# Transposes of two batches moved to SyncE's DMA queue, under a new written order

## The chip, the cores and the metric

The kernel runs on one core of one Trainium2 chip. The metric is the device time of one execution in microseconds: 173.79 us before the change (median of 3 runs, 173.76 to 174.22). Engines: PE is TensorE's matmul, PEld its weight load, DVE is VectorE, ACT is ScalarE, POOL is GpSimd, SP is SyncE. SyncE computes nothing here; all loads and stores are issued on its queue (SPq).

## The reference

Four batches, 8 heads, 768 positions, 48 values a head. A gated linear recurrence is followed by a mixer with a low-rank position part and a channel part:

```python
for t in range(S):                                   # per batch and head, state is 48 x 48
    state = alpha[:, :, t, :, None] * state + np.einsum('bhd,bhe->bhde', k[:, :, t], v[:, :, t])
    y[:, :, t] = np.einsum('bhd,bhde->bhe', q[:, :, t], state)
x = y as (4, 768, 384)
h = xt @ U @ V                                       # xt: x transposed, U 768 x 32, V 32 x 768
u = x + h.transpose(0, 2, 1)
out = u + np.maximum(u @ w_ch1, 0.0) @ w_ch2         # w_ch1 384 x 1536, w_ch2 1536 x 384
```

Inputs and output are float32; the kernel multiplies in bfloat16 and sums in float32 in PSUM.

## The kernel before

A batch's 768 positions are cut into six chunks of 128. Batch 0 and the first four chunks of batch 1 go through `stage_pair`, which takes two chunks together by halves of the heads; the last two chunks of batch 1 and all chunks of batches 2 and 3 go through `stage_gla`. One chunk in `stage_gla` runs like this:

- Four loads of 192 KB (alpha, k, q, v) into four of 36 `io` buffers, each load in runs of 192 bytes (L347).
- ScalarE takes the logarithm of alpha (L543). PE forms its cumulative sum over the chunk (L550) and the chunk's total (L552). ScalarE takes exponentials of minus and plus the sum, `ai` and `aa` (L560, L561), and of the total, `tot` (L563).
- GpSimd makes `rk` = k times `ai` and `rq` = q times `aa` (L570), 128 positions by 8 heads by 64 columns in bfloat16 (48 used, the rest zero), and casts v to `rv`.
- PE transposes `rk` and `rq` in four 128 x 128 blocks each (L583) into one PSUM bank each, and ScalarE or VectorE copies the banks to `kt` and `qt` in SBUF (L590).
- PE forms the scores from `kt` and `qt` (L608), VectorE masks them to `pm` (L618). PE forms the chunk's own state (L631), VectorE adds the previous state and VectorE or GpSimd scales the sum by `tot` (L658, L642).
- PE forms the output from `qt` with the previous state and from `pm` with `rv` (L670, L675), and it is copied to `xb`.

After six chunks `stage_mix` makes the low-rank part (L691, L722) and transposes the sum `ub` for the channel part (L732). `mlp1` multiplies by the first weight matrix in 24 groups of three matmuls a batch (L759), each group followed by the maximum with zero on ScalarE or VectorE into `h1t` (L769, L771). `mlp2` multiplies by the second, for each chunk in three groups of four matmuls (L782); then VectorE adds `ub` into one of four `ou` buffers (L789) and SyncE stores it (L790). PE groups of one batch's channel part stand between those of the next batch's recurrence.

The order of all work is written out by hand in `TABLE`: three characters an entry, two for the operation and one for its engine. `Plan.run` walks the table, binds a buffer to each operation that needs one (that which the plan takes to come free first), and issues the operation on the engine named. Each engine runs its own entries strictly in this order, and waits at an entry until its inputs and its buffer are there. The costs in `Plan.add` (`{"SP": 1100.0}`), `LAT` and `lag` serve only to estimate when buffers come free, and to decide how many idle matmuls (L286, `filler`) are put between PE's groups in the first 28 us. They choose buffers and do not delay anything.

`QUEUE_T` is a list of (batch, chunk) whose transposes are done by a transfer instead of PE. It is empty before the change; the code for it issued on ScalarE's queue.

Of the kernel before, what the change touches and what calls it, by code (L numbers as in the profile page):

```python
# [20 lines left out]
BdSAgSBeSBbSAmSA0SAsSGMGANGAJGALGAVGBgSAXGDRDDXDAuSAySCrPAwSD8ADvPBfSAqSBkSA2SCtDCsDDSDD+PEQPDzABlSDwAEIAESAEADD-DEBPEWP
EPPERAECPEXPBhSBmSDYPETPGLADxAEYDEDDGNPEEPDaAGhAG3AEVDEUDEZPEFDDZDGOAEGAEbAEaDG5PEcPEdPBiSEeDEfPEiPGjPBjSEuPElPEvPEjPErP
EmPG7AG6AGPAG8AHOAGQAEwAEsPGSDE3PEoPGUPEgPE4DBnSEpPGWDGRDBsSEkAEtAE7PHQPBoSEqAEnAHTAHRAGkAE8DGlAE1PE5PFpPE6DFqAHSAEhDFnP
GTPFdPFPPFRPFQAFSAGnDFeDFDPGVDEzPFHPGmAFIAGXPGoDFoDGaPE0DGbDGcDFbPFFPGpPGqPGsAGrAFEDFcDE2DAjGG+GGYDG9DGZDFfPFgAFVPFZPFTP
FrPAZGFGAGiAFXPE-PFWAFUDFaAFYDFsDGePGwPGtPE9PGgDFAAE+AG4AGxDGyDGuDFJPFjPHUDFNPHAPFBPGzDHCAGfDGvDAnGFKAFkAFCAHVGFlPAlAHlA
AhGApGG-PFhPHXPHBDG0PHGPAzGAvGFmDA1GArGHZAFOAAtAGdDG1AHHDF3PFLPFMAFiDHIDHJDG2AHWPFyPHYDHaPHDPAxAHnPA3GHPAFzPF4PHrAH7AHoA
HpAH9PH+AIAGHqAHEDHcDHbDHFDF8PH-AHdPHLPF0PF5PHsGIBGHtGHNDHeDHfDF1DHgDF6DHmGHKGHuPICPF9PIDPGBPHhDIEDIFAHwDHMDHvPHiPIGPHxD
HyPGCPHkAH8GHjDKBAJtAH0DHzDH1PH3DH2DH4GGGPGDPH5PF+PKDPIIDIHDIJPGHPJvPIKABpSJxAJzAJwABqSKFAH6DF-DGEDB0SF2SBvSBwSJyABrSF7S
B8SB1SBtSB2SBxSBzSBySILPBuSIMDExPFtPJ0GJ1GEyDITPIVPINPIbPGIPIPPJuGIWDFuPIZPIUDIODIQDIXPIRPIcDIaDISDFvPIdPJ2PIYAIfPIhPIzP
KEAIeAKrAKHAKWAFwDKGAI0AJ4DIgDJHPJ3PKtPJDPJIAI5PJ5DGJDKvALVAJ9PKYPIrPKxAKuAKwAJ+DKCGKIGKzGKXGI3PJ6PI6DJEDIiAKaAKZAI7PJFP  # L30
I-PKcAKbAJ8DI4DJ7DKRPI9PI8DI+AJ-PKdGJNPInPJGDJADKSDJODIsAKKPJLPItPJMAKMAIuDKTDLXPK1PIxPKyGKeGK3DLZAKJGLYAJBPKmPIjPJCAKAA
IpPIkDIoDK0PKfPKgPJjPKLPJkPK2DKhAIyAIqAKiDKnDKNAK4PK5DK6DKjPKOPJoPB3SB4SB9SJJPB+SGKSCASB5SLAAB6SGASJKAKPDKlDKoDKkDLaGKsG
LbGB7SCFSCISB-SCESLCPJpPIlPJlPJqPLGALEALFALDAImDJmDKQDLHGLdPJePLIGLfALcPK7PK+PI1PKUPK8DI2AKVDLJPJfPLKPKpPNHALeAKqALLDK-A
JrDLMDK9GLBGJgPNJPLQPLgPLNPLRDLODLPDLiDJUPIvPJZPJVPLTPLSGLWGLhDLjPNwANbAIwDLUDLkANyPJaPNdPLlPNhANfANLANeANNANKANMANzAJnS
JsSCGSCCSNjGCBSCQSN1ACDSGFSN0AN2ANgALmDCJSJbPJPPJcDJhDLtPCKSCMSCUSCHSNPGNiGCWSCPSCLSCNSNOGNIGN4GN3GNcGJQPLnPOGGLvPJWPLpP
LuDLoDLwDLzPL1PNlPLqDLxPNRPLrPJRPL0DL2DLsANkPL3PNQPLyDNmDMLPL4DNTDNnANSAJSDMNPL5PNXPMPPMVPMODL6DNYDMQAMMAOaAMWAOvACVSCOS
CRSNUPNoPNWDMdPMDPNqDNpDN5PL-PMhPMEDMeAOFAMAAMiDNVDOxPOHPOcPN7AOzAOeAOyAOdAOfAN6PMRPMJPMHPN8DMKAOJAOKANrPMXPOgAOIAMSDMYD
MIDNsDNxGOLAMnPO1GL7PL9PNtDL+AN9PL8AMBPMfPNZPO3PN+DN-DMoAO5DNaDOAPNuPMFPODPMCANvAMgAMGDOBDOCDOEDCSSJiSO0GOMGONGOhGOVPMuP
O2POPPOOPMvPMZPOiGOjPORAO4AOQAMaAOkPOWDJXDMTPOlDOmDO6POSPOnPMUAMwPJTSCTSCXSObGOXDOqPO8DOpDOrDOTDOoDO7DMzPMbPM0PMxDOUDOsG
OwGM4POtPNCPO9POYPO+AMlPMjPOuDOZAMcAO-PMkAMmDM5PPAAMpPPHPPBPPJPPNPMqPM1PPCDPIDPDPPKDPODPPPPEDNDPPLPFxSMySPQDJYSPFPM6PPRP  # L40
# [128 lines left out]
def kernel(  # L169
# [164 lines left out]
    def stage_loads(b):  # L334
        def load(t, src, c, key):
            if paired(b, c):
                hs, sl = slice((c % 2) * HP, (c % 2 + 1) * HP), slice((c // 2) * 2 * C, (c // 2 + 1) * 2 * C)
# [9 lines left out]
            P.add({"SP": 1100.0}, lambda e: nc.sync.dma_start(t(), src[b, :, sl, :].rearrange("h t d -> t h d")), w=[t], prio=key)  # L347
# [427 lines left out]
    def mlp2(b, ub, h1, c):  # L775
# [13 lines left out]
        P.add({"DVE": 468}, lambda e: nc.vector.tensor_tensor(ou(), ub()[:, c, :], hb()[:, 0:DM], op=ALU.add), r=[hb, (ub, c)], w=[ou], prio=-100)  # L789
        P.add({"SP": 550.0}, lambda e: nc.sync.dma_start(out[b, c * C : (c + 1) * C, :], ou()), r=[ou], prio=-1)  # L790
# [53 lines left out]
```

## Time and profile before

| | |
|---|---|
| median of 3 runs | 173.79 us |
| the profiled execution, its own time | 173.62 us |
| its span | 171.8 us |
| PE busy | 156.7 us, 91% of the span |
| DVE, ACT, POOL busy | 117.6, 89.5, 62.4 us |
| DMA queue of the loads and stores | 28.52 MB in 87104 packets, 66.2% of 16 engines |
| last matmul ends | 161.0 us |

The time is about 1.8 us above the span, which runs from the first to the last instruction. "Busy" of PE counts pipelined matmuls with modelled ends. A stage view gives the busy time of each engine between two points of the span; a chain row gives a start, a length and the work that ended the wait before it.

### The profile page before, as it was taken

The numbers are of one execution on the slowest core, as the hardware profiler recorded it, in microseconds if no ns is written. First come the engines' busy times: TensorE is split into PE (matmuls) and PEld (weight loads), VectorE is DVE, ScalarE is ACT, GpSimd is POOL, SyncE is SP. The second block draws the span as 40 slices with busy tenths as digits, with TensorE's granted clock in tenths as the row PEclk, the third lists the DMA queues.
The fourth block names the chain that finished last, engine by engine and source line by source line (L and its number), as shares of the span: only waits on it lengthen the run. The fifth ranks groups of instructions, "written<-read, shape, count | busy, mean of one in ns | idle before, by whom it ended". The sixth has DMA issues, their size and how long they took to land.

```text
span 171.8 us, 4668 instructions
## 1 busy us (share of the span) xinstructions
PE 156.7 (91%) x1814; PEld 102.8 (60%) x1814; DVE 117.6 (68%) x257; ACT 89.5 (52%) x226; POOL 62.4 (36%) x101
## 2 busy tenths in 40 slices
...
GB/s 135 283 303 311 259 287 270 320 349 325 291 179 196 218 236 177 222 255 173 59 50 132 237 164 191 239 191 4 0 92 4 90 1 0 4 137 0 47 92 183
DMA packets 87126, 28.81 MB, mean 168 GB/s; under 512 B 80928, under 2 KB 87072, under 8 KB 87104
## 3 DMA queue, kind: packets, MB, share of 16 engines
q1 hardware_dynamic: 87104, 28.52, 66.2%
...
q14 instruction: 8, 0.07, 0.1%
HBM read 23.79 MB, written 4.72 MB: 166 GB/s over the span
## 4 chain that ended last, share of the span: by engine, by line
PE 79%; DVE 9%; DMA 5%; issue 2%; SPq 1%; ACT 1%; DVEq 0%
PE ps L782 28%; PE ps L759 22%; PE ps L583 4%; PE ps L415 3%; DMA io<-in_alpha_dram 3%; PE ps L722 2%; DMA out_dram<-ou 2%; DVE pm L453 2%; PE ps L608 2%; PE ps L442 2%; DVE h1t L771 2%; PE ps L732 2%; PE ps L675 2%; PE ps L528 1%; PE ps L550 1%
## 5 line engine op out<-in xcount | busy, mean ns | idle before, releaser
L782 PE MATMUL ps<-w_sb,h1t 128*128 128x384 bf16 x288 | 54.2, 326 | 0.0
L759 PE MATMUL ps<-uT,w_sb 128*128 128x384 bf16 x288 | 53.0, 326 | 0.2 <-DVE pm L453 0.2
L759 PEld LDWEIGHTS <-w_sb 128*128 128x128 bf16 x288 | 26.7, 98 | 16.1 <-issue 0.3
L782 PEld LDWEIGHTS <-h1t 128*128 128x128 bf16 x288 | 26.2, 98 | 15.7 <-issue 0.6
L769 ACT ACTIVATE h1t<-ps 128x384 bf16<-128x384 f32 x56 | 25.4, 503 | 19.0 <-PE ps L759 17.0
L771 DVE TENSOR_SCALAR h1t<-ps 128x384 bf16<-128x384 f32 x40 | 20.9, 550 | 12.4 <-PE ps L759 12.2
L789 DVE TENSOR_TENSOR ou<-ub,ps 128x384 f32<-128x384 bf16 x24 | 12.5, 548 | 14.8 <-PE ps L782 11.9
L570 POOL TENSOR_TENSOR rk<-io,ai 128x384 bf16<-128x384 f32 x14 | 13.0, 939 | 16.9 <-ACT ai L560 16.9
L618 DVE TENSOR_TENSOR pm<-ps,maskc 128x512 bf16<-128x512 f32 x28 | 18.0, 683 | 1.5 <-PE ps L608 1.5
L570 POOL TENSOR_TENSOR rq<-io,aa 128x384 bf16<-128x384 f32 x14 | 12.9, 928 | 8.5 <-ACT aa L561 8.5
L297 POOL CAST w_sb<-io 128x384 bf16<-128x384 f32 x21 | 11.9, 591 | 7.7 <-DMA io<-in_moe_w_ch_dram 5.3
L293 ACT CAST xb<-ps 128x192 bf16<-128x192 f32 (+1 forms) x18 | 6.8, 397 | 14.5 <-PE ps L675 13.2
L723 DVE TENSOR_TENSOR ub<-xb,ps 128x384 bf16<-128x384 bf16 x24 | 11.9, 548 | 3.2 <-PE ps L722 3.0
L453 DVE TENSOR_TENSOR pm<-ps,maskp 128x512 bf16<-128x512 f32 x20 | 13.0, 680 | 1.0 <-PE ps L442 1.0
L293 ACT COPY qt<-ps 128x512 bf16<-128x512 bf16 x12 | 8.2, 682 | 9.2 <-PE ps L583 5.9
L297 POOL CAST rv<-io 128x384 bf16<-128x384 f32 x17 | 8.7, 513 | 5.0 <-DMA io<-in_v_dram 5.0
L293 ACT COPY uT<-ps 128x768 bf16<-128x768 bf16 x5 | 4.0, 799 | 9.1 <-PE ps L732 9.0
L293 ACT COPY kt<-ps 128x512 bf16<-128x512 bf16 x13 | 7.5, 588 | 1.2 <-PE ps L583 0.9
L642 POOL TENSOR_TENSOR st<-sm,tot 128x384 bf16<-128x384 f32 x4 | 3.3, 831 | 12.4 <-DVE sm L658 12.4
L295 DVE CAST xb<-ps 128x192 bf16<-128x192 f32 (+1 forms) x16 | 6.6, 423 | 1.6 <-PE ps L528 1.0
L286 PE MATMUL ps<-filler 128*128 128x512 bf16 x20 | 6.5, 461 | 1.2 <-DVE filler L217 1.2
L372 ACT ACTIVATE lt<-io 128x384 bf16<-128x384 f32 x10 | 5.0, 535 | 4.2 <-DMA io<-in_alpha_dram 4.2
(116 smaller groups left out, 252.7 us busy)
## 6 DMA issues: line engine op xcount, KB each, us to landing
io<-in_q_dram SPq DMA_DIRECT2D x24, 192.0 KB, 4.1
io<-in_alpha_dram SPq DMA_DIRECT2D x24, 192.0 KB, 3.9
io<-in_v_dram SPq DMA_DIRECT2D x24, 192.0 KB, 3.7
io<-in_k_dram SPq DMA_DIRECT2D x24, 192.0 KB, 4.1
io<-in_moe_w_ch_dram SPq DMA_DIRECT2D x24, 192.0 KB, 4.1
out_dram<-ou SPq DMA_DIRECT2D x24, 192.0 KB, 2.1
...
```

The lines of the kernel that those rows point to most:

```text
L293: nc.scalar.copy(dst, src)
L297: nc.gpsimd.tensor_copy(dst, src)
L453: nc.vector.tensor_tensor(dst, s2, maskp.to_broadcast([C, 2, 2, C]), op=ALU.mult)
L570: eng.tensor_tensor(dst()[:, :, 0:D], a(), x(), op=ALU.mult)
L583: nc.tensor.matmul(t[:, p, :], lhsT=ring()[:, 2 * p : 2 * p + 2, :].rearrange("t h w -> t (h w)"), rhs=ident, start=True, stop=True, is_tr ...
L618: nc.vector.tensor_tensor(pm()[:, :, par, :], s2, maskc.to_broadcast([C, HP, C]), op=ALU.mult)
L723: P.add({"DVE": 465}, lambda e, c=c, hb=hb: nc.vector.tensor_tensor(ub()[:, c, :], xb()[:, c, :], hb()[:, 0:DM], op=ALU.add), r=[hb] + xk( ...
L759: nc.tensor.matmul(hb()[:, 0:TW], lhsT=w1_sb[:, ct, jt * 128 : (jt + 1) * 128], rhs=uT()[:, ct, tt * TW : (tt + 1) * TW], start=(ct == 0), ...
L769: nc.scalar.activation(dst, hb()[:, 0:TW], AF.Relu)
L771: nc.vector.tensor_scalar_max(dst, hb()[:, 0:TW], 0.0)
L782: nc.tensor.matmul(hb()[:, 0:DM], lhsT=h1()[:, jt, c * C : (c + 1) * C], rhs=w2_sb[:, jt, :], start=(jt == 0), stop=(jt == NJ - 1),)
L789: P.add({"DVE": 468}, lambda e: nc.vector.tensor_tensor(ou(), ub()[:, c, :], hb()[:, 0:DM], op=ALU.add), r=[hb, (ub, c)], w=[ou], prio=-100)
```

## The change

The rows of `TABLE` are all new. `QUEUE_T` names the twelve chunks of batches 2 and 3, and for each of them two transposing transfers (`rk` to `kt`, `rq` to `qt`, each 128 x 512 values) are issued on SyncE's queue, in place of two PE groups of four transposes and two copies out of PSUM. `Op` gets a field `iss`, the queue time that the plan books for an entry on SyncE, and some planning figures of loads and stores differ. The new table has 24 entries more on SyncE and 48 fewer on PE, ScalarE and VectorE together.

```diff
 TABLE = """
-A6SA4SA8SBASBESABSA+SA-SA9SA5SBISBMSBGSA7SBCSBFSBHSBBSBDSBKSBJSCuACYACaPBNSBOSBLSCwPADGDbADEACbACdACyAC1DDGPDdPAEPCxACcA
...
+A4SBASBA6SBBSBYSA7SA5SA8SBCSA9SBESBaSA-SBZSBDSA+SBISABSBGSBMSBFSBHSBNSBOSBJSBKSBLSCYADEADGPCaPBPSDIACZGCcACdAG3ADHACbADJA
...
-    __slots__ = ("engs", "fn", "prio", "deps", "bufs", "n", "users", "est", "i", "mode", "lag")
+    __slots__ = ("engs", "fn", "prio", "deps", "bufs", "n", "users", "est", "i", "mode", "lag", "iss")
...
             if eng == "SP":
-                dma = max(dma, t + 600.0) + cost
-                clock[eng] = max(t + 550.0, dma - 3500.0)
+                dma = max(dma, t + op.iss + 30.0) + cost
+                clock[eng] = max(t + op.iss, dma - 3500.0)
                 end = dma + 2000.0
...
-    QUEUE_T = ()
+    QUEUE_T = tuple((b, c) for b in (2,3) for c in range(6))
...
-                    {"SP": 775.0},
+                    {"SP": 690.0},
...
-            P.add({"SP": 1100.0}, lambda e: nc.sync.dma_start(t(), src[b, :, sl, :].rearrange("h t d -> t h d")), w=[t], prio=key)
+            P.add({"SP": 930.0}, lambda e: nc.sync.dma_start(t(), src[b, :, sl, :].rearrange("h t d -> t h d")), w=[t], prio=key)
...
         if (b, c) in QUEUE_T:
             for dst, src in ((kT, rk), (qT, rq)):
-                P.add({"ACT": 100}, lambda e, dst=dst, src=src: nc.scalar.dma_start_transpose(dst(), src().rearrange("t h w -> t (h w)")), r=[src], w=[dst], prio=pr + 18, lag=2600)
+                P.add({"SP": 450}, lambda e, dst=dst, src=src: nc.sync.dma_start_transpose(dst(), src().rearrange("t h w -> t (h w)")), r=[src], w=[dst], prio=pr + 18, lag=-700.0, iss=1250.0)
...
-        P.add({"SP": 550.0}, lambda e: nc.sync.dma_start(out[b, c * C : (c + 1) * C, :], ou()), r=[ou], prio=-1)
+        P.add({"SP": 550.0}, lambda e: nc.sync.dma_start(out[b, c * C : (c + 1) * C, :], ou()), r=[ou], prio=-1, lag=-1500.0)
```

Where the text speaks of the written order, these parts of the two tables are meant (each entry: batch, chunk; for the matmuls of `mlp2` also the group, 0 to 2; line numbers are those of the kernel before, from L44 on one more than in the changed file):

| | before | after |
|---|---|---|
| PE's last groups of `mlp2` | ... 3,2 g1; 3,5 g1; 3,4 g1; 3,2 g2; 3,0 g1; 3,5 g2; 3,0 g2; 3,4 g2 | ... 3,1 g1; 3,0 g0; 3,4 g2; 3,1 g2; 3,5 g0; 3,0 g1; 3,3 g1; 3,3 g2; 3,0 g2; 3,5 g1; 3,5 g2; 3,2 g1; 3,2 g2 |
| VectorE's last additions L789 | 3,4; 2,4; 3,1; 3,3; 3,0; 3,2; 3,5 | 3,4; 3,1; 3,0; 3,5; 3,3; 3,2 |
| SyncE's last stores | 3,4; 3,0; 3,1; 3,5; 2,4; 3,2; 3,3 | 2,4; 3,1; 3,4; 2,0; 3,0; 3,5; 3,3; 3,2 |
| SyncE's entries from the third load of batch 2 on | 46 loads, 9 stores up to the last load | 45 loads, 8 stores, 24 transfers up to the last transfer |
| PE groups between the cumulative sum and the scores of 3,4 | 12 of L759, 2 of L782, 16 of the recurrence | 3 of L759, 7 of L782, 7 of the recurrence |

More of the change, by code (lines that the diff above doesn't have):

```diff
@@ L16 @@
 TABLE = """
-A6SA4SA8SBASBESABSA+SA-SA9SA5SBISBMSBGSA7SBCSBFSBHSBBSBDSBKSBJSCuACYACaPBNSBOSBLSCwPADGDbADEACbACdACyAC1DDGPDdPAEPCxACcA
-C3PBPSC5DCfDC0GCeGCzACvABQSBYSBUSAaSChPAGPC2PDIADeADJAAFADHADyADgADfACgPAHDC9PD0PCjDC+DCiDC4AEHADiGCZGC6PAcSAASBSSASSBcS
-AQSAeSCnPDkPC-PDhGAOSBRSC7DCoDDADC8DDKGDFGD1AD2ADmADcAD3ACkPCpPDjPDqPEJPDlADrPDLDClDCqDDsDCmDD5DDBPELAEKADCAEMADMPDtPDNP
-DnPD4GDTPEOGENGDDADuDDpDDUPD7PDVDDoDDOADPAD9ADQPDWPD6PACGAISBWSAbGBVSBTSAMSAYSAKSAfGAdGAkSAWSBXSBZSATGARGAPGAUSBaSAiSAoS
@@ L21 @@
[L21 to L40, printed above, removed]
@@ L41 @@
-PGAPMDNEPPSAPjPPXPPvPMrPPzPM7DM2DNFDNGSM3SP0APwAP9PPhPP3PP7PPZPP+APaDPiDPkAPVPPrPPnPP5PPsAPWDP6AP4APoAP8AQBPPTPPbPPlPPxP
-PtPPyDQCAPUAPcDPuDM9PPfPPpPP-PM+PPdPQADPmAPYAP1PM-PQNPP2APeDPgDMsDQIPQJPPqAQXPQDPQSPQKPQTPQcPQUPMtSM8SJdSQOPQdPQYPQPPQEP
-QePQFPQZPQaDNADQLDQVDQbSQGDQHSQMSQQDQfDQgSNBSQRSQWS
+A4SBASA6SBBSBYSA7SA5SA8SBCSA9SBESBaSA-SBZSBDSA+SBISABSBGSBMSBFSBHSBNSBOSBJSBKSBLSCYADEADGPCaPBPSDIACZGCcACdAG3ADHACbADJA
+CfGCuADKDCeDG5PCnPChPG6ADLGDMPCgPDOAG7AG8ACwPCxACzACyADbACvABQSC0GG9GCjDCoDCiDBcSBUSDFGCpPDNPCkPCqDClDG+DDPDCmDDdPHAPC9P
@@ new lines @@
+DQPC2PC1GADGC+DDeAHCADRDDgADfAC4AG-PHBDDTPC-PDUPHDPC3PDyADiGDhGDcGDVDDADC5ADSDHEDEHADWPD0PCrPDXDCsDC6PHFDC8DC7DEJPDYPD3A
+D1AD2AELAEKAEMAEOGD5GCtADzGEIGDjPAEPDkPDqPAFADlDDaDENDDrPDBPDsDEPPDtPEQPDmADZADDADCAESADnPD4DERDDuDD6PD7PD8AD9AEBPEWPGLA
+ECPETPHOADpDDoDEDDEXPDvPD+PEVDEUDGNPBSSAYSAASBVSBRSBXSAUSDxAGhAHQPGjPACGGiGAZGBTSAWSGMGAVGAXGGQAEYDGPADwAGOAEADD-DEZPGSD
+EEPEbDEaDEGDGRDHSAGlAEFAGUPAGPEcPEdPGkAAHAGmAEeAHTAGWDGnDEuPEoPEfPGTPErPAOSBeSAQSEzPE0DASSBdSAKSAMSBWSAaSBfSAISEsPElPBbS
+AeSBkSBgSEmPAcSAiSAsSBhSAmSBjSHRAGVAEtDBiSAqSAkSAgSBmSBlSAoSAuSBoSA0SEgPEvPAwSBnSA2SBsSAySEpPEiPEjPGXPEwDEnAEhAEqAEkDGaP
@@ new lines @@
+GwPGxDGbDGpPFlPFjPGZDFhPGcDGYDFmAGrAFkAARGATGAPGALGANGAbGGdDAJGFNPFJPFiDGyDHVDFODExPFLPFdPFbPHXPFHPFFPFMAHUDFeAFGAFKDFcA
+GoDEyDFIDFDPE7PHWPE-PGqPFXPE9PFAAFEDGsAHPGGzGG4GHYDHZDFYAE+AE8DAfGHdPGePHeDHGPGgDHHDHlAGfDHfGHIDAdGHgDFBPFfPHnPFgAFCAHJD
+HaPGtPGuDHhDGvDFnPFZPFVPFTPAjGHoAH7AHpAFaAH9PFrPFUAHqAHKGHmGHbDFoDHcDFPPFpPFRPE5PFsDHtGHsGFQDE6DH-AH+AHrAAnAFWAArGG0PHLP
+HiPG2DHkDHNDG1DFSAIBGIAGAlAAhAHMAHjAH8GHuPHvPE1PH1PF8PIDPF3PH3DE2DHxAFqDH2DHwAICPGBPFyPIFAApAAtAJtAAvAH4DIEDJ-AIGPHyPF4P
+H0DGCPFzPJvPF9PIHDHzDIIDH5PH6DIJPAzAA1GA3GAxGJwAIKDGGPKBPGDPILPBpSBqSBtSB0SB1SBwSBuSKDAJzAJyAKEAKCAGEDIMAKFAJxAF0PF+PKSA
@@ new lines @@
+F1DIVPITPJ0GJ1GKGGIZPIPPKHGIWDIbPGHPF5PIUDINPBySB4SB8SJ2SF2SB2SCASJ3SIaDIcDF6DIQDIXPFtPE3PIdPFuPKJSB5SBxSBvSIYAKlAIeAIOD
+GIPFvPGJDI3PIRPKnPKUPI-PKpAKqAK4ALLAKWAKrAKoAKXAJAAKVAKYAF7SKISBrSISDI4DFwDE4DJBPJNPIhPInPIpPKaGKsGKtGKZGJuGKAGJDPM7AIoD
+JODIiDIqAJEALNPIrPI5PIfPIgDIsDF-DI6AJCDJJPK6PIvPLOAK7ALPAJHPI7PI9PJKAJIAI8AI+AKKPJ4PIwDCESKcSKuSB+SB9SBzSKbSB6SKvSGKSKMD
+J5DKLDJ6DB3SIzPIxPJLPJFPJ7PItPI0AJGAIuAJ8DJMDK+AK9ANNAJePIlPKNPJoPKQPJ9PImDKRAK8AJ+DJfPJgPKODKdPKwPIyAK-GLQGKTGLAGLRGKmG
+LBSB7SCMSJhDCBSM9PKgPJjPKeDKPDKfDKxDKhDKyDLSSCCSLCSLTSKiDIjPJkPNBAM+AIkANPPKzPJUPI1PK5GNCGM-ANAANzAK0DJpPK2PJqPLGPN1PJVP
@@ new lines @@
+K1DLHDI2ANRAK3ANQANTANSALDPB-SNDGLIDLUPLMGGFSCISCFSNESNFSJiSLEDLFDJlPJWPLVDKjPLJPLWDJZPLXPJmDLKDJaPLYDKkAN5ANgAN4AJrDN2A
+N3ANiPLZPNGPCUSJPPNUGNmANkALaANlANjAOZALdPLhPLpPJQPNIDNHDCNSCDSCGSLnPLiDLqDLoDLjPLkDCVSCWSJsSJnSGASCKSCQSCHSJbPObPLrPLlP
+JRPLbPLmDLeDN6GOcALsANVGM8GLcDN8SMPPMLPMZPMQDLfPOdAMMDLgDOeGNoGOfGCOSNWSNXSNOGN7GNJPMNPMHPJXDLzPCJSNKDCLSJSDMJPL9PL+AMOA
+L0DL7PMaDL8DL5PMFPJcDMGDLvPL1PMbPMRPL2AL6ALxPNYPMIALyAMKDLwDOGANZDL3PNbPMXPNLPMTPL4AMcANMANcDNaDNnGLtPCSSOgSOhSNqSCRSMYD
+L-PNhGMUDNePOIPMBPN9SMSDOKAOJANuPMDPLuDOLAMCAMdPNfAMnPMePOMAMEAMAANdGNvDNpSCTSOOGONGNwGOiPN+PCPSNrPOHGMoPOkDNtDOjDOQSNsD
@@ L44 @@
+OPSCXSMiPMjPMVPOADN-DNxPOUPN0GOBPOCDNyAMWAMpPORPM2PODDOSDOVDOTDJTSJYSFxSJdSOWDOaGM3POEPMsPOXPOlPOmAOFAMqDOYDMkPMxPOnPMlD
+OoDMfPMtPOpPOrPOqDO3POxPOyDOsDMuPOvPOwDMyPO1POtPOuAOzPO2DO4DM4PO5PO0DMvDO6DMzPO-PO9PMwSM5DM0DPAAO+APVPPdPPTPMmSMrSPPPPBP
+PHPM6SPQAPCAPRPPeDPIDPbPPSAPUAPcAO7PPDPPWDPEAPlPPFPPnPPZPPfPPNPPoAO8APGAPaDPgAMgDPwPPpPP1PPXPPjPPYDPqDPkDPmDPJPPLPPhPP6P
+P-PPOAPKAPiDPMDQAPPxPPrPQBPPyPQEPPsPP7PP8PPtPQFPQGPP2PP3PQCDPzDM1SP0SQDSMhSPuDPvSQHDP9DQISP+SP4DP5S
 """
@@ L86, in __init__, with add @@
         self.readers = {}
-    def add(self, engs, fn, r=(), w=(), prio=0.0, mode="F", lag=0.0, after=()):
+    def add(self, engs, fn, r=(), w=(), prio=0.0, mode="F", lag=0.0, iss=570.0, after=()):
         op = Op()
-        op.engs, op.fn, op.prio, op.mode, op.lag = engs, fn, prio, mode, lag
+        op.engs, op.fn, op.prio, op.mode, op.lag, op.iss = engs, fn, prio, mode, lag, iss
         op.i = len(self.ops)
```

## The prediction

> **What bounds the kernel now.** I read the page's head and engine line first, then the busy time by stage, cut at the first channel-mixing matmul (31.13 us) and at the end of the last one (161.01 us), and last the chain that ended last.
>
> ```profile
> span 171.8 us, 4668 instructions
> PE 156.7 (91%) x1814; PEld 102.8 (60%) x1814; DVE 117.6 (68%) x257; ACT 89.5 (52%) x226; POOL 62.4 (36%) x101
> ```
>
> ```profile
> 0.00:31.13 31.13, 27.26 (x450) 18.03 (x450) 22.15 (x64) 23.96 (x63) 15.88 (x36) 1.00 0.98 263
> 31.13:161.01 129.88, 129.40 (x1366) 84.81 (x1364) 91.98 (x189) 65.56 (x165) 46.55 (x65) 1.00 0.62 148
> 161.01:171.80 10.79, 0.00 (x0) 0.00 (x0) 3.52 (x7) 0.00 (x0) 0.00 (x0) 0.66 0.35 128
> ```
>
> Columns: stage, its length, busy PE, PEld, DVE, ACT, POOL, granted clock, DMA share, GB/s. In the middle stage TensorE is busy 129.40 of 129.88 us at full clock while no other engine passes 92: there PE work is time, one for one. The last stage has no PE work at all, and it lasts 10.79 us. The chain says why:
>
> ```profile
> 137.08 7.80 PE ps L759 x48
> ...
> 148.62 12.36 PE ps L782 x76
> 161.01 0.57 DVE ou L789
> 161.59 2.19 DMA out_dram<-ou
> 163.87 0.56 DVE ou L789
> 164.45 1.83 DMA out_dram<-ou
> 166.37 0.56 DVE ou L789
> ```
>
> All 76 last matmuls run before any of the seven pending additions `ou`: VectorE takes them in the written order, and the first of them belongs to chunk 4, whose last group is written last on PE. With four `ou` buffers, seven additions need two store landings in between. So the kernel is bound by PE work for 130 us and by a chain of additions and stores for the last 11. The profiled execution took 173.62 us, 1.82 above its span; the median of the runs is 173.79 (0.1% more). I sum against 173.62. About 0.3% is what a measurement of this kernel can tell from no change.
>
> **The change part by part.**
>
> *Transposes off PE.* Twelve chunks lose two PE groups of four, 96 matmuls of L583.
>
> ```profile
> L583 PE MATMUL ps<-ident,rk 128*128 128x128 bf16 x56 | 5.1, 219 | 0.0
> L583 PE MATMUL ps<-ident,rq 128*128 128x128 bf16 x56 | 5.4, 219 | 0.0
> ```
>
> ```profile
> 54.20 0.45 PE ps L583 x8
> ...
> 118.28 0.67 PE ps L583 x12
> ```
>
> The 219 ns are the pipelined length of one; the chain shows what one costs in a stream: 0.45/8 = 0.67/12 = 56 ns. 96 x 0.056 = 5.4 us, all in the stage where PE is the bound: **-5.4 us**.
>
> The Trainium skill, "VectorE: DVE Perf Modes", section "The three transpose paths", gives 390 ns for a 128x128 bf16 transpose on TensorE and 1309 ns by the DMA crossbar. By its first figure the 96 would give back 37 us; the rows show 56 ns each, and the measurement decides. Its second figure speaks against the change and returns among the rivals.
>
> *Evictions gone.* With them go 24 copies of kt and qt out of PSUM.
>
> ```profile
> L293 ACT COPY kt<-ps 128x512 bf16<-128x512 bf16 x7 | 4.0, 586 | 0.9 <-PE ps L583 0.9
> L293 ACT COPY qt<-ps 128x512 bf16<-128x512 bf16 x5 | 3.0, 591 | 5.9 <-PE ps L583 5.9
> ```
>
> These are ScalarE's twelve of the copies from 50 to 122 us. At 0.59 us each that is 24 x 0.59 = 14 us off engines that are not the bound. PE covers it, and its idle time in the middle stage is only 129.88 - 129.40 = 0.5 us. I take 0, with 0 and -0.5 as ends.
>
> *The tail.* In the new order PE's last groups are: chunk 5 twice, chunk 2 twice, each group four matmuls of L782 (12.36/76 x 4 = 0.65 us). VectorE's last additions are chunks 4, 1, 0, 5, 3, 2, in nearly the order in which PE ends them, and SyncE stores each behind its addition.
>
> ```profile
> L789 DVE TENSOR_TENSOR ou<-ub,ps x7: 547/549/555, 161.0 to 166.8; 128x384 f32<-128x384 bf16 x7
> L790 SPq DMA_DIRECT2D out_dram<-ou x7: 332/423/462, 161.6 to 168.8; - x7
> ...
> DMA to landing us min/median/max: 1.8/1.9/2.2
> ```
>
> Let T be PE's end. Chunk 5 is complete at T-1.30; its addition and that of chunk 3 behind it take 2 x 0.55 and end near T-0.15. Chunk 2 ends at T, its addition at T+0.6, its store goes out at once (0.42 us each; the two before it are out by T+0.4). From the last store's issue to the end of the span it now takes 171.8 - 168.8 = 3.0 us. So the tail is 0.6 + 0.05 + 3.0 = 3.65 instead of 10.79. The buffers do not stand in the way: chunk 1 is complete nine groups before PE's end, at T-5.9, so its store goes out near T-5 and lands within 2.2 us, ahead of the addition of chunk 5 at T-1.25. **-7.1 us**.
>
> *24 transfers on SyncE.* No row shows a transposing transfer. Issue first:
>
> ```profile
> L347 SPq DMA_DIRECT2D io<-in_q_dram x14: 391/916/1857, 46.5 to 108.3; - x14
> L347 SPq DMA_DIRECT2D io<-in_v_dram x14: 384/656/1336, 49.1 to 112.2; - x14
> ...
> L790 SPq DMA_DIRECT2D out_dram<-ou x24: 332/424/1471, 56.1 to 168.8; - x24
> ```
>
> Columns: least, median and longest ns on SyncE's queue. The ends for one issue are 0.33 and 1.86 us. I take 1.0, nearest to the 0.92 of the q loads, whose runs are short like the 256-byte blocks of a transposed tile. Between the first load of batch 2 (44 us) and the last scores less a landing (about 116 us) the queue has 72 us. The new order puts 45 loads and 8 stores there: 45 x about 0.72 (three parts 0.656, one part 0.916) + 8 x 0.42 = 36 us. That leaves 36 us for 24, 1.5 us each: at 1.0 it fits, at 1.86 it would be 9 us over.
>
> Then the data, 128 KB each:
>
> ```profile
> 60.00:80.00 20.00, 20.00 (x201) 13.14 (x198) 15.89 (x33) 12.46 (x33) 9.93 (x14) 1.00 1.03 214
> 80.00:100.00 20.00, 20.00 (x247) 13.80 (x246) 15.21 (x31) 10.83 (x30) 7.63 (x11) 1.00 0.58 128
> 100.00:120.00 20.00, 19.77 (x227) 13.76 (x225) 17.96 (x35) 13.23 (x35) 11.19 (x15) 1.00 0.75 159
> ```
>
> At the 214 GB/s of the full stretch one takes 0.61 us, at the stage rate of 263 GB/s 0.50; 24 take 12 to 15 us. The DMA engines idle 0.42 x 20 + 0.25 x 20 = 13.4 us between 80 and 120 us. So it fits, but only just, and batch 2's twelve fall where the share is already 1.03: they push loads of batch 3 back by 6 to 7 us into that idle time.
>
> What waits: on SyncE a transfer waits for POOL's rk or rq, and behind it stand loads and stores. A late store holds an `ou` buffer and with it VectorE; a late transfer stops PE at its scores, as PE takes its groups in order too. The tightest place in the written order is chunk 4 of batch 3. (The row of waits has the total, the times and the longest in us.)
>
> ```profile
> L570 POOL TENSOR_TENSOR rk<-io,ai 128x384 bf16<-128x384 f32 x14 | 13.0, 939 | 16.9 <-ACT ai L560 16.9
> L560 ACT ACTIVATE ai<-ps 128x384 bf16<-128x384 f32 x14 | 7.0, 507 | 0.1
> POOL rv L297 <- DMA io<-in_v_dram: 5.0, 4, 2.3
> ```
>
> ```profile
> io<-in_q_dram SPq DMA_DIRECT2D x24, 192.0 KB, 4.1
> ...
> out_dram<-ou SPq DMA_DIRECT2D x24, 192.0 KB, 2.1
> ```
>
> Between its cumulative sum and its scores PE has seven groups of L782 (7 x 0.65), three of L759 (9 x 7.80/48 = 1.46) and some small ones: about 7 us of cover. Needed: one exponential (0.51), two products on POOL (2 x 0.94), two issues partly behind them, then a landing. With a store's 2.1 us that is 0.5 + 1.9 + 1.0 + 2.1 = 5.5, no stall; with a load's 4.1 it is 7.5, a stall of 0.5. The other chunks have more between. Over all I take **+1.5 us** of stalls (three such chunks at 0.5), ends 0 and 8 (twelve chunks at 0.65, the step from a 2.1 to a 4.1 landing and a queue at 1.5).
>
> *The first 31 us.* The loads' order is new; three loads of batch 1's chunk 2 stand ahead of batch 0's last. At 0.5 to 0.66 us an issue that is up to +2; against it, that work can fill PE where it now runs idle matmuls:
>
> ```profile
> L286 PE MATMUL ps<-filler 128*128 128x512 bf16 x20 | 6.5, 461 | 1.2 <-DVE filler L217 1.2
> ```
>
> I take 0, ends -1.5 and +1.5.
>
> **Sum:** 173.62 - 5.4 - 7.1 + 1.5 = **162.6 us**.
>
> **The rivals.**
>
> *Late landings.* The transfers queue behind loads at a full DMA share, and most chunks of batches 2 and 3 stall 0.3 to 0.9 us. For it: shares of 1.03 and POOL's four waits for v loads (5.0 us) show loads that now arrive just in time. Against: 13.4 us of idle DMA follow. Time: 162.6 - 1.5 + 5 to 11 = 166 to 172. Chance 0.14.
>
> *SyncE becomes the bound (slower than before).* Place: its queue from 44 to 116 us. If one transfer holds the queue longer than 1.5 us, each further us costs 24, as loads and stores wait behind; the 11.0 us of gain are eaten at 1.5 + 11/24 = 2.0 us. At 2.5 us: 162.6 + 24 = 187. For it: single loads hold the queue up to 1.86 us. Against: the medians are 0.42 to 0.92. Chance 0.07.
>
> *The DMA engines become the bound.*
>
> ```profile
> q1 hardware_dynamic: 87104, 28.52, 66.2%
> ```
>
> A packet costs an engine 0.662 x 171.8 x 16 / 87104 = 20.9 ns now. If the transpose cuts 128 KB into packets of 32 bytes, 4096 of them on 16 engines take 5.35 us; 24 take 128, of which 13.4 find idle engines: 162.6 + 115 = 277 us. Nothing in the trace shows such packets, and nothing excludes them. Chance 0.03. The skill's 1309 ns for a 128x128 block by the crossbar, named above, gives 4 x 1.309 = 5.2 us a transfer, an estimate, if blocks go one after another: the same case. No run so far shows it.
>
> *The tail stays.* If the additions again bunch behind PE's end, say because VectorE is late with the last `h1t`, the 7.1 us do not come: 169.7. For it, that VectorE holds 41 of the 96 `h1t` evictions in the new order; against, its share in the last 20 us of PE work is low. Chance 0.03.
>
> **How the numbers follow.** Forecast case, 159 to 166: 0.70. Late landings 0.14, tail 0.03, below 159 0.01 (no stall and a better start): faster 0.88. Stalls that just cancel: same 0.02. SyncE 0.07 and DMA 0.03: slower 0.10. The range 159 to 170 takes in the start's and the stalls' ends (162.6 - 1.5 - 1.5 and 162.6 + 6.5 + 1.5, cut a little) and leaves out 0.16.
>
> **What would show it.** Right: L583 at x16 for each of rk and rq; PE still near full from 31 us to its end; from PE's end to the span's end 3 to 4 us; SyncE's transfers near 1 us. Wrong: idle PE before L608 with a transfer as releaser, loads of batch 3 that land late at POOL, issues above 1.5 us, or a DMA share of 1.0 up to 120 us.

## The result, and the profile after

The changed kernel takes 178.55 us (median of 4 runs, 177.96 to 179.01) beside 173.92 of the kernel before: the ratio is 1.026, 95% interval 1.022 to 1.030. Forecast was 162.6. The change is slower, and the forecast had the wrong sign. Ratios, here and below, are to the kernel before on the same chip and leave out runs in a slower state of the chip, so where a median and a ratio do not fit exactly, the ratio is the better one.

The page's head, the queue's row, and busy time by stages of 20 us (the columns are those of the prediction):

```profile
span 176.2 us, 4488 instructions
PE 154.9 (88%) x1713; PEld 97.9 (56%) x1714; DVE 114.3 (65%) x247; ACT 83.7 (47%) x211; POOL 61.2 (35%) x102
...
q1 hardware_dynamic: 100160, 31.67, 78.4%
```

```profile
60.00:80.00 20.00, 19.76 (x176) 12.39 (x175) 11.13 (x22) 13.26 (x36) 8.46 (x12) 1.00 0.99 202
80.00:100.00 20.00, 15.50 (x166) 9.70 (x165) 13.19 (x24) 8.24 (x24) 7.11 (x11) 1.00 1.06 170
100.00:120.00 20.00, 16.85 (x172) 10.79 (x173) 14.01 (x28) 6.70 (x17) 7.20 (x9) 1.00 0.92 195
120.00:140.00 20.00, 16.46 (x181) 10.33 (x179) 11.97 (x22) 7.06 (x18) 7.66 (x12) 1.00 0.82 164
```

The last of these stages in the kernel before:

```profile
120.00:140.00 20.00, 20.00 (x195) 12.87 (x194) 11.96 (x24) 6.62 (x14) 1.28 (x2) 1.00 0.11 41
```

The stage in which PE had 0.5 us of idle time before now has 11 us of it between 80 and 140 us alone, and the DMA engines no longer rest there: shares of 1.06, 0.92 and 0.82 stand where 0.58, 0.75 and 0.11 stood. The end, by contrast, is as forecast. From the chain that ended last:

```profile
162.05 10.41 PE ps L781 x64
172.46 0.02 issue
172.49 0.56 DVE ou L788
```

PE ends at 172.46, the span at 176.2: a tail of 3.7 us (3.65 was forecast, 10.79 before). If the forecast gains of 7.1 and 5.4 us came, the 4.4 us of longer span hide a loss of about 17. Who waits, from the waits (total us, times, longest):

```profile
POOL rv L296 <- DMA io<-in_v_dram: 24.9, 11, 4.1
...
POOL rk L569 <- DMA io<-in_k_dram: 12.6, 6, 3.9
...
POOL rq L569 <- DMA io<-in_q_dram: 10.2, 6, 2.6
...
PE ps L607 <- DMA qt<-rq: 8.2, 5, 2.8
```

Loads come late, GpSimd waits for them, and PE waits at its scores for transfers that wait for GpSimd. The transfers' own rows (least, median, longest ns on SyncE's queue):

```profile
L593 SPq DMA_TRANSPOSE kt<-rk x12: 1205/1309/1842, 69.1 to 135.2; - x12
L593 SPq DMA_TRANSPOSE qt<-rq x12: 1205/1216/1574, 72.4 to 133.6; - x12
...
DMA to landing us min/median/max: 2.4/3.2/5.0
```

The time for which one entry occupies the queue is called its hold here. No transfer's is below 1.2 us. On the DMA engines they cost 0.784 x 176.2 - 0.662 x 171.8 = 24.4 us, 1.0 us each; the prediction had 0.5 to 0.6. The 13,056 packets more are 544 a transfer, and with 3.15 MB more they hold 241 bytes each on the mean.

### The profile page after: what moved, and what is told of

The parts are those of the page before. It is cut to its first block, busy times and chain, and to the rows that moved or that the text cites. A ratio compares the mean times of both kernels' runs of the same rounds, so it can differ in the third digit from the quotient of the medians.

```text
span 176.2 us, 4488 instructions
## 1 busy us (share of the span) xinstructions
PE 154.9 (88%) x1713; PEld 97.9 (56%) x1714; DVE 114.3 (65%) x247; ACT 83.7 (47%) x211; POOL 61.2 (35%) x102
## 4 chain that ended last, share of the span: by engine, by line
PE 40%; DMA 18%; DVE 4%; SPq 3%; issue 2%; POOL 1%; ACT 0%; POOLq 0%; DVEq 0%
PE ps L781 19%; PE ps L758 13%; DMA qt<-rq 6%; DMA out_dram<-ou 6%; DMA io<-in_k_dram 2%; SPq L346 2%; DMA io<-in_q_dram 2%; DVE ou L788 2%; PE ps L607 2%; PE ps L721 1%; DMA kt<-rk 1%; PE ps L731 1%; SPq L593 1%; DVE pm L617 1%; DVE ub L722 1%
## 5 line engine op out<-in xcount | busy, mean ns | idle before, releaser
L758 PE MATMUL ps<-uT,w_sb 128*128 128x384 bf16 x288 | 51.8, 326 | 2.1 <-DVE ou L788 2.1
L770 DVE TENSOR_SCALAR h1t<-ps 128x384 bf16<-128x384 f32 x41 | 20.9, 548 | 9.2 <-PE ps L758 6.6
L788 DVE TENSOR_TENSOR ou<-ub,ps 128x384 f32<-128x384 bf16 x24 | 13.1, 550 | 19.1 <-PE ps L781 10.1
L569 POOL TENSOR_TENSOR rq<-io,aa 128x384 bf16<-128x384 f32 x14 | 12.7, 912 | 22.4 <-DMA io<-in_q_dram 10.2
L296 POOL CAST rv<-io 128x384 bf16<-128x384 f32 x23 | 11.6, 510 | 25.2 <-DMA io<-in_v_dram 24.9
L569 POOL TENSOR_TENSOR rk<-io,ai 128x384 bf16<-128x384 f32 x14 | 12.8, 913 | 18.0 <-DMA io<-in_k_dram 12.6
L607 PE MATMUL ps<-qt,kt 48*128 48x128 bf16 x112 | 5.2, 217 | 9.2 <-DMA qt<-rq 8.2
L542 ACT ACTIVATE lt<-io 128x384 bf16<-128x384 f32 x14 | 7.3, 531 | 6.9 <-DMA io<-in_alpha_dram 6.9
L607 PEld LDWEIGHTS <-kt 48*128 48x128 bf16 x112 | 3.3, 94 | 12.5 <-issue 6.7
L560 ACT ACTIVATE aa<-ps 128x384 bf16<-128x384 f32 x14 | 6.9, 496 | 6.0 <-PE ps L551 4.3
L296 POOL CAST w_sb<-io 128x384 bf16<-128x384 f32 x17 | 8.5, 523 | 3.4 <-DMA io<-in_moe_w_ch_dram 3.4
L562 ACT ACTIVATE tot<-ps,off 128x4 f32<-128x4 f32 x22 | 5.7, 279 | 5.8 <-DVE st L641 5.4
L559 ACT ACTIVATE ai<-ps 128x384 bf16<-128x384 f32 x14 | 7.0, 499 | 1.7 <-PE ps L551 1.7
```

Of the source, the lines that this page charges most:

```text
L296: nc.gpsimd.tensor_copy(dst, src)
L542: P.add({"ACT": 435}, lambda e: nc.scalar.activation(lt()[:, :, 0:D], at(), AF.Ln), r=[at], w=[lt], prio=pr + 40)
L569: eng.tensor_tensor(dst()[:, :, 0:D], a(), x(), op=ALU.mult)
L607: nc.tensor.matmul(sc[par]()[:, p * C : (p + 1) * C], lhsT=kT()[o : o + D, p, :], rhs=qT()[o : o + D, p, :], start=(p == 0), stop=(p == HP ...
L758: nc.tensor.matmul(hb()[:, 0:TW], lhsT=w1_sb[:, ct, jt * 128 : (jt + 1) * 128], rhs=uT()[:, ct, tt * TW : (tt + 1) * TW], start=(ct == 0), ...
L770: nc.vector.tensor_scalar_max(dst, hb()[:, 0:TW], 0.0)
```

## The experiments

Line numbers follow each kernel.

**Is the new order bad, or are the transfers?** `g_no_transfers` leaves them out.

```diff
-... lambda e, dst=dst, src=src: nc.sync.dma_start_transpose(dst(), src().rearrange("t h w -> t (h w)")) ...
+... lambda e, dst=dst, src=src: None ...
```

> The changed kernel with its 24 transfers left out (kt and qt of batches 2 and 3 keep old values; every other entry of the written order stays). Theory Q (the 24 transfers are the cost: they hold SyncE's queue 1.2 to 1.8 us each and take about 1 us of all 16 DMA engines each): nothing else is wrong with the new order, so the sum of the prediction without stalls holds: 173.6 - 5.4 - 7.1 = 161, at most 163. Theory O (the new order is itself worse: its loads are 1.5 MB behind at 44 us, before any transfer is issued, and PE starves later for that): still 168 or more, with POOL waiting for k, q and v loads as in the changed kernel.

Measured: 161.84 us, ratio 0.931 (0.927 to 0.936). PE is busy 80.00 of 80 us from 60 to 140. So the 24 transfers account for the loss of 16.7 us, and the rest of the new order for none of it.

**Their price, or their place?** `h_plain_copies` puts plain copies of the same bytes at the same places, with the same waits.

```diff
-nc.sync.dma_start_transpose(dst(), src().rearrange("t h w -> t (h w)"))
+nc.sync.dma_start(dst().rearrange("x e c -> x (e c)"), src().rearrange("t h w -> t (h w)"))
```

> The 24 transposing transfers replaced by plain copies of the same 128 KB from rk or rq to kt or qt (the transposition is left out), at the same places of the queue and with the same waits. Theory Q1 (the price of a transposing transfer is the cost: an issue of 1.2 to 1.8 us and 1.0 us of the DMA engines): a plain copy issues in about 0.5 us and takes about 0.3 to 0.6 us of the engines, so most of the loss goes: 163 to 167. Theory Q2 (it is the place in the queue: an entry that waits for POOL with loads behind it, and a landing of 3 us before the scores, whatever is sent): 173 or more. Theory O: 170 or more.

Measured: 162.40 us, ratio 0.936 (0.930 to 0.942). Places, waits and a landing behind the queue cost 0.6 us in all, less than the intervals of the two ratios: theory Q1. What a plain copy costs, by the queue's row of the page and by the transfers' own rows:

```profile
q1 hardware_dynamic: 90560, 31.66, 77.7%
```

```profile
L593 SPq DMA_DIRECT2D kt<-rk x12: 471/670/1962, 64.6 to 117.0; - x12
L593 SPq DMA_DIRECT2D qt<-rq x12: 540/600/1058, 67.3 to 116.1; - x12
...
DMA to landing us min/median/max: 2.1/2.7/3.8
```

About half the hold (0.6 to 0.67 us), and 0.777 x 159.6 less the 114.6 us of the run without transfers (0.713 x 160.7), 9.4 us or 0.4 a transfer on the engines. Two prices differ; the next runs take them one at a time.

**The hold alone.** `i_held_queue` and `j_held_once` put two tiny transfers, or one, ahead of each plain copy.

```diff
+    def held(dst, src):
+        for _ in range(2):          # j_held_once: range(1)
+            nc.sync.dma_start(tiny.pop(), tsrc[0:16, 0:4])
+        nc.sync.dma_start(dst().rearrange("x e c -> x (e c)"), src().rearrange("t h w -> t (h w)"))
```

> As the run with plain copies (162.4 us), with two tiny transfers (16 partitions, 8 bytes each, from a constant to places of their own) ahead of each of the 24 copies: they hold SyncE's queue about 0.3 to 0.4 us each, so that one place costs 1.3 to 1.4 us there as a transposing transfer does, and hardly load the DMA engines. Theory S: 172 or more. Theory D: 162 to 165. If both this and the run with short runs stay near 163, neither price alone makes the loss, and it takes both or the later landing.

Measured: 193.36 us, ratio 1.107 (1.100 to 1.114). The two tiny ones hold more than meant, 0.59 us each, and a place costs 1.7 us, more than a transposing transfer. The DMA share from 60 to 140 us is only 0.69, so the queue alone can do it. With one:

> As the run with two tiny transfers ahead of each plain copy (193.4 us, 0.59 each beside 0.53 for the copy: a hold of 1.7 us a place), with one of them: a hold of about 1.1 us a place, just under the 1.2 to 1.3 of a transposing transfer, at the DMA price of a plain copy (0.4 us of all engines). If the queue alone makes the loss of the changed kernel: 174 to 178. If the time on the DMA engines is needed as well: 164 to 171; the run with short runs (0.8 us of the engines, 0.7 us of hold) gave 168.7.

Measured: 177.35 us, ratio 1.010 (1.006 to 1.015). The entries on the queue, and a stage of 20 us:

```profile
L361 SPq DMA_DIRECT2D kt<-rk x12: 524/526/541, 67.8 to 133.0; - x12
...
L360 SPq DMA_DIRECT2D tiny<-tsrc x24: 549/641/1260, 66.9 to 132.3; - x24
```

```profile
80.00:100.00 20.00, 16.64 (x172) 10.00 (x167) 12.13 (x22) 7.95 (x22) 8.49 (x11) 0.91 0.70 159
```

A hold of 0.64 + 0.53 = 1.17 us a place by the medians (1.29 by the mean, beside 1.33 for the transposing transfers) brings most of the loss: 13 to 15 us more than the plain copies alone, by ratio or by median, at a DMA share of 0.70 where PE starves. The granted clock is 0.91 in that stage, but the run of this kernel with a clock of 1.00 took 176.0 us, so the clock is not what makes the loss. So the hold suffices for most of it.

**The engines alone.** `p_short_runs` copies only the 48 used columns of each head, in 1024 runs of 96 bytes.

```diff
+nc.sync.dma_start(dst().rearrange("x e (s w) -> x (e s) w", w=64)[:, :, 0:D], src()[:, :, 0:D])
```

> As the run with plain copies (162.4 us), but each of the 24 copies moves only the 48 used columns of each head, in 1024 runs of 96 bytes (transposition left out). At the 20.9 ns a packet of the kernel before that is about 1.3 us of all 16 DMA engines a transfer, more than the transposing transfer's 24.4/24 = 1.0, while the issue should stay near that of a load, 0.5 to 0.7 us. Theory D (time on the DMA engines is the price): 172 or more. Theory S (the hold on SyncE's queue, 1.2 to 1.8 us a transfer, is the price): 162 to 165.

Measured: 168.72 us, ratio 0.964 (0.958 to 0.970), between what the two theories gave. The queue's row and the transfers':

```profile
q1 hardware_dynamic: 112064, 30.88, 80.5%
```

```profile
L593 SPq DMA_DIRECT2D kt<-rk x12: 605/754/1037, 66.5 to 124.4; - x12
L593 SPq DMA_DIRECT2D qt<-rq x12: 601/684/1046, 69.4 to 123.4; - x12
```

(0.805 x 166.5 - 114.6)/24 = 0.8 us of the engines at a hold of 0.7: it costs 6.9 us. The packets came cheaper (12.4 ns each) than the 20.9 ns that I had reckoned. So time on the engines counts too, for less.

**Relief from both.** `e_long_runs` keeps the transposing transfers and makes the loads of batches 2 and 3 cheap.

```diff
-nc.sync.dma_start(t(), src[b, :, sl, :].rearrange("h t d -> t h d"))
+nc.sync.dma_start(flat(t), src[b].rearrange("h t d -> (h t d)")[c * C * DM : (c + 1) * C * DM].rearrange("(p f) -> p f", f=DM))   # b >= 2
```

> The changed kernel, with the loads of batches 2 and 3 read in runs of 1536 bytes instead of 192 (the same amount of data from the wrong places, so the values are permuted). That takes packets off the DMA engines (48 x 1024 runs become 48 x 128) and leaves the transposing transfers and their 1.2 us of issue as they are. Theory D: the DMA share from 60 to 140 us falls well below 0.95, the loads no longer come late, 162 to 166. Theory S: the loads stand behind 24 x 1.3 us of issue all the same, 172 or more.

Measured: 164.93 us, ratio 0.945 (0.941 to 0.950). It would speak for theory D, but the loads hold the queue less as well:

```profile
L346 SPq DMA_DIRECT2D io<-in_k_dram x14: 378/430/758, 41.8 to 115.1; - x14
L346 SPq DMA_DIRECT2D io<-in_v_dram x14: 328/481/1991, 42.9 to 123.0; - x14
```

(0.43 and 0.48 us; 0.67 and 0.58 in the changed kernel.) It shows that a transfer's 1.2 us and its landing near 3 us are harmless once queue and engines have room; it does not tell the two apart.

**The queue of ScalarE.** `d_act_queue` issues the transfers there (`nc.scalar` for `nc.sync`).

> The 24 transfers issued on ScalarE's queue instead, at the same places of the written order. Theory S (SyncE's time and order: 24 x 1.3 us of issue and its waits for POOL, behind which the loads stand): loads run ahead again, POOL's waits for k, q and v shrink, 164 to 172 in spite of what ScalarE loses. Theory D (the DMA engines: 24 x 1.0 us more at a share of 1.0): the share from 60 to 130 us stays at 0.9 to 1.0, and the time at 175 or more; ScalarE's own work, 1.2 us a transfer later, can add some us in both.

Measured: 179.81 us, ratio 1.024 (1.015 to 1.032), no better. It frees SyncE, but leaves the engines' price and puts the waits for GpSimd into ScalarE's order, ahead of its exponentials and evictions. The waits of the profiled execution (180.62 us):

```profile
POOL rv L296 <- DMA io<-in_v_dram: 14.1, 6, 4.1
...
ACT h1t L768 <- DMA kt<-rk: 6.5, 1, 6.5
ACT aa L560 <- DMA qt<-rq: 5.8, 1, 5.8
```

The sign of theory S did come: GpSimd's waits for k, q and v loads (L569 and L296) fell from 47.7 us in the changed kernel to 15.3. But ScalarE now stood behind the transfers instead. It speaks against moving the hold there as a cure; what each part weighs it cannot say.

**The waits for GpSimd.** `f_const_source` lets the transfers read a constant tile.

> The changed kernel, with the 24 transposing transfers reading a constant tile instead of rk and rq (so the scores of batches 2 and 3 are formed from zeros): issue and DMA price stay, but no transfer waits for POOL on SyncE's queue and none holds an rk or rq buffer. Theory W (waits in the queue: a transfer that waits for POOL, whose input is a load that stands behind it or lands late): 163 to 168. Theory D or S (price of the transfers): 172 or more, with POOL still waiting for k, q and v loads.

Measured: 176.96 us, ratio 1.012 (1.007 to 1.016). Theory W falls as the main cause: waits for inputs, and `rk` and `rq` buffers held by transfers, are about 2 us of the loss.

**The price in quiet.** `q_alone` appends 24 transfers to the kernel before, behind its last store.

> The kernel before with 24 transposing transfers from a constant tile appended after its last store, where the DMA engines are idle (their results go nowhere). It prices one transfer by itself: theory of the engine: the queue still holds 1.2 us each and the DMA share of the stretch is at 0.8 to 1.0, as a transfer is bound by its 544 packets; theory of contention: the share is near 0.5 (0.5 to 0.6 us of the engines each), and the 1.0 us in the changed kernel comes from the loads beside them. The span grows by 24 x 1.2 = 29 us.

One run: 205.53 us; its stretch of transfers alone, and the rows on the queue:

```profile
172.00:202.00 30.00, 0.00 (x0) 0.00 (x0) 0.00 (x0) 0.00 (x0) 0.00 (x0) 0.50 0.49 100
```

```profile
L817 SPq DMA_TRANSPOSE kt<-tsrc x12: 1205/1264/1282, 170.1 to 200.2; - x12
L817 SPq DMA_TRANSPOSE qt<-tsrc x12: 1211/1264/1265, 174.1 to 196.3; - x12
```

The hold stays 1.26 us with nothing but these transfers in flight: it does not come from loads beside them. The engines are half idle meanwhile: 0.49 x 30/23 = 0.6 us a transfer, about as the theory of contention had it. The difference of whole pages that gave 1.0 us in the changed kernel gives (0.645 x 203.8 - 113.7)/24 = 0.7 us here; the rest comes in company with the loads.

**The tail alone.** `t_tail` is the kernel before with the end of `TABLE` reordered: PE's last groups by chunk, additions and stores in the order of completion.

> The kernel before with only its end reordered: the last PE groups by chunk, with chunk 5 last, and the last additions and stores in the order in which PE completes the chunks. No transfer, all else as before. The prediction's term of the tail: -7.1 us, span's end 3.7 us after PE's, so 166 to 167.5. Rival: another wait at the end (a late h1t, PSUM banks) eats it: 171 or more.

Measured: 166.29 us, ratio 0.957 (0.954 to 0.959); run again, 165.97 and 0.956 (0.953 to 0.959).

```profile
148.18 12.36 PE ps L782 x76
160.54 0.02 issue
160.57 0.56 DVE ou L789
```

The same 76 matmuls, and one addition behind them. The span is 164.0: a tail of 3.5 us.

**The order with transposes on PE.** `a_order_pe` and `k_batch3_queue` set PE's transposes at the places of the transfers.

> The new order with all transposes on PE (at the places of the transfers). By the sum of the prediction: 161.8 + 96 x 0.056 = 167.2, within 1, so that the order is worth about 6.5 us against before, all of it at the tail. If the transposes' PSUM banks or copies stand in the way of this order: 169 or more.

> The changed kernel with batch 2 transposed on PE again (two groups of four transposes and two copies out of PSUM a chunk, at the places of the transfers in the order) and only batch 3's 12 transfers on SyncE's queue. If the queue's time is what runs out (36 us free for 24 places, so the first 12 at 1.25 fit), the loss vanishes but for single late landings: 164 to 168, that is the 161.8 of the run without transfers and 2.7 us of transposes and up to 3 of stalls. If every transfer costs its share of the loss: about 161.8 + 2.7 + 16.7/2 = 173.

Measured: 176.29 us (1.010, 1.006 to 1.013) and 174.10 (0.991, 0.987 to 0.996). The first was 9 us above its forecast. Neither settles it: at these places PE itself waits for rk and rq, and has 7.4 us of idle time from 40 to 160 us in `a_order_pe`. Set about 2.5 us of PE work ahead of the scores, with five buffers each for rk and rq:

```diff
+    rq_s = slots("rq", 5, [C, H, 64], BF16)
+    rk_s = slots("rk", 5, [C, H, 64], BF16)
```

> The new order with all transposes on PE, this time about 2.5 us of PE work ahead of the scores (in a_order_pe they stood at the places of the transfers, where PE waited for rk and rq: 2.0 us at L583 alone, and 3.0 us idle from 60 to 80 us), with five buffers each for rk and rq in place of four and three, which have to live longer now. By the sum of the prediction: 161.8 to 162.4 + 96 x 0.056 = 167 to 168. If the order itself starves PE when its transposes take PE's time: 172 or more.

Measured: 169.39 us, ratio 0.972 (0.967 to 0.976), some 2 us above the forecast, with 2.7 us of idle time in the same stretch. Then half on the queue:

> As a2_order_pe_late for batch 2, batch 3's 12 transfers on SyncE's queue. Theory of the queue (about 7 us free there, a plain copy's 0.65 us hold was absorbed 24 times, so 12 x 1.26 = 15 us is absorbed too, as 24 x 0.65 = 15.6 was): a2's time less 2.7 us, 164 to 166. If each transfer brings its own stall, a late landing ahead of PE's scores, whatever the queue's load: a2's time plus 2 to 6, 168 or more.

> The other half: batch 2's 12 transfers on SyncE's queue, batch 3 transposed on PE as in a2_order_pe_late. Theory of the queue: 164 to 167 as for the other half; slower than that half by up to 3 us if it is the loads of batch 2 and 3 standing behind the transfers that count, since batch 2's transfers have more loads behind them.

Measured: 166.93 us (0.959, 0.955 to 0.963) with batch 3's transfers, 173.82 (0.999, 0.996 to 1.002) with batch 2's. The stage from 80 to 100 us of `a2_order_pe_late`, of batch 3's half and of batch 2's half:

```profile
80.00:100.00 20.00, 19.32 (x248) 13.45 (x241) 16.09 (x30) 11.08 (x31) 8.13 (x10) 1.00 0.79 164
```

```profile
80.00:100.00 20.00, 19.77 (x260) 13.68 (x257) 16.36 (x31) 11.53 (x33) 9.04 (x11) 1.00 0.72 151
```

```profile
80.00:100.00 20.00, 16.75 (x172) 10.21 (x171) 11.99 (x22) 8.18 (x22) 8.18 (x11) 0.91 1.04 165
```

Batch 3's twelve give back the 2.5 us of 48 transposes (2.7 by the sum) and cost nothing more; batch 2's twelve, with the loads of batches 2 and 3 behind them and the engines at 1.04, cost 4.4 + 2.7 = 7.1 us. The same number of transfers, another place.

**Six late transfers in the old order.** `v_tail_six` is `t_tail` with `QUEUE_T = ((3, 0), (3, 1), (3, 2))`, each transfer right behind its product.

> The kernel before with its end reordered as in t_tail (166.3 us), and the transposes of the first three chunks of batch 3 as six transfers on SyncE's queue, each right behind the product that it reads (14.7 and about 7 us of PE work ahead of the scores). Theory of the queue (what counts is loads standing behind the transfers; six holds of 1.3 us fit where the queue waits anyway, for stores, after 80 us): 166.3 less 24 transposes x 4... that is 24 x 0.056 = 1.3 us: 164.5 to 165.5. If a transfer costs its hold wherever it stands: 166.3 - 1.3 + 6 x 0.6 = 168 or more.

> The same kernel as t_tail, to compare with the run beside it on the same chip: 166.3 us within 0.5.

Measured: 177.54 us, ratio 1.022 (1.019 to 1.026), beside 165.97 without the six. That is 12 us above the range of the first theory, and on the side of the second (168 or more), but 9.5 us above the sum by which it got there. The queue's entries in order of time, its wait, and the stage:

```profile
91.90 1.16 SPq L347 DMA_DIRECT2D io<-in_q_dram  x2
99.28 1.29 SPq L594 DMA_TRANSPOSE qt<-rq  x1
```

```profile
SPq L594 <- POOL rq L570: 8.3, 2, 7.0
```

```profile
100.00:120.00 20.00, 9.72 (x76) 5.75 (x75) 7.93 (x16) 4.83 (x13) 5.72 (x9) 0.76 0.88 177
```

The first transfer waited 7.0 us for rq, and SyncE issued nothing from 93.06 to 99.28. The loads behind it came that much later, then the products made from them and the transfers of those, and PE stood for 10 us, 9.4 of them in one wait for a `kt`. This is my placing and not the changed kernel's, where the constant source showed 2 us; it shows what one entry that waits costs on a queue that also carries the loads.

## Why the prediction was wrong

*The tail* (-7.1): right. 3.7 us in the changed kernel; alone, `t_tail` gained 7.4 to 7.8 us.

*The transposes off PE* (-5.4): right as far as tested. Half of them were worth 2.5 us (169.39 to 166.93) where queue and engines had room.

*Evictions and start* (0): within their bounds; the run without transfers came out at 161.84 where the sum without stalls was 161.1.

*The step that failed: the time that SyncE's queue has for 24 transfers.* I gave it 72 us, from what I took for the first load of batch 2 in the old order (44 us) to 116, took 36 off for 53 plain entries at their median hold, and found 1.5 us free for each transfer. The window was the first mistake. The line of these loads also serves the last two chunks of batch 1, and the k loads at 44 us are theirs. The loads and stores counted here begin 8 us later, in the old order too:

```profile
44.14 2.29 SPq L347 DMA_DIRECT2D io<-in_k_dram  x2
...
52.55 0.66 SPq L347 DMA_DIRECT2D io<-in_k_dram  x1
...
111.73 1.16 SPq L347 DMA_DIRECT2D io<-in_v_dram  x2
```

So the trace of before already showed 46 loads and 9 stores taking 60 us, up to 112.9, with one wait of 6.6 us for an addition among them. In the new order weights fill the queue for longer; the first of those 45 loads (k of chunk 0) is issued at 58.75 us. The changed kernel, and then the run without transfers:

```profile
57.68 0.98 SPq L311 DMA_DIRECT2D io<-in_moe_w_ch_dram  x1
...
58.75 0.39 SPq L346 DMA_DIRECT2D io<-in_k_dram  x1
...
135.18 1.21 SPq L593 DMA_TRANSPOSE kt<-rk  x1
136.44 0.58 SPq L346 DMA_DIRECT2D io<-in_v_dram  x1
```

```profile
55.50 0.99 SPq L311 DMA_DIRECT2D io<-in_moe_w_ch_dram  x1
56.58 0.39 SPq L346 DMA_DIRECT2D io<-in_k_dram  x1
...
109.01 2.29 SPq L789 DMA_DIRECT2D out_dram<-ou  x4
```

Without transfers the 53 plain entries and the last load take from 56.6 to 109.0, 52 us, 1.0 us each and not 0.68. To 116 us that left 7 us, not 36. The holds come to 44 us (a mean of 0.82, where the prediction took medians), the waits for `io` buffers and for additions to 8. That loads hold longer because the DMA engines are at 0.96 there is argued, not shown; `e_long_runs`, with fewer packets, had shorter holds. With transfers the same part of the queue takes from 58.75 to 137.0, 78 us: 26 more, for transfers that hold it 32 us (24 at a mean of 1.33). The prediction sized one transfer at 1.0, inside its bounds, and mis-sized the room by far more.

*The DMA price* (12 to 15 us into 13.4 idle): mis-sized. It was 24.4 us; 0.6 to 0.7 us a transfer alone, 1.0 beside loads. Counted on the engines, 52.4 x 0.96 = 50 us of plain work and 24 us of transfers come to 74, and 78.3 x 0.95 is 74 too. So queue and engines ran out together. The runs show that the hold suffices for most of the loss, and that 0.8 us on the engines at a short hold makes 7 us. How the 16.7 us would divide if only one of them were cured stays open; moving the hold to ScalarE cured nothing, and the new order with all 24 transfers placed later was not run.

*The stall at chunk 4 of batch 3* (+0.5, three such): the wrong place. From 60 us on, PE first stands idle near 80 us, for 1.4 us, behind an addition that waits for a store; then at 89 to 92 us, at scores of batch 2, for transfers that were issued late. No single landing is to blame: the transfer that it waited for last there was issued at 88.78 and had landed by 91.94, near the median of 3.2 us, and plain copies with a landing of 2.7 us cost 0.6 us in all. Of the signs named for being wrong, idle PE at the scores, late loads at GpSimd and a DMA share near 1.0 up to 120 us all came.

*The rivals.* "SyncE becomes the bound" was the case that came, at its place and with its mechanism, but its points of decision hung on the same 36 us: full at 1.5 us a transfer, the gain eaten at 2.0. 0.07 was too little. With the room that the run without transfers shows, 7 us plus the 9 by which plain copies lengthened the queue without harm, the queue is full near 16/24 = 0.7 us, and the gain is eaten near 0.7 + 11/24 = 1.1. Worked out afterwards, 24 x (hold - 0.7) fits three runs by their mean holds: 15 us at 1.33 for the changed kernel (16.7 measured), 14 at 1.29 for `j_held_once` (13 to 15), 30 at 1.96 a place for `i_held_queue` (31). `p_short_runs` at 0.76 lost 5 us more than it gives, which is what time on the engines alone can be seen to add. "The DMA engines become the bound" had packets of 32 bytes; they hold 241 on the mean, and it came in at about a fifth of that price (24.4 us, not 128).

The Trainium skill, "VectorE: DVE Perf Modes", section "The three transpose paths", gives the 1309 ns of the rival for one 128x128 block. Four blocks in one transfer took 1.31 us back to back (24 in 31 us), so here the time fits the whole transfer and not a block. The Trainium skill's "DMA: Bandwidth & Descriptors", section "Issuing engines are not separate DMA queues", says that the sequencer's time to initiate is usually small relative to the DMA itself. Here it is not small: 1.2 to 1.3 us of hold against 0.6 to 1.0 us of engines, or against 2.4 us at the least from issue to landing. The part of that rule which expects little from spreading transfers over queues agrees with `d_act_queue`.
